# A planned attention and gated feed-forward kernel: load order of the first chunk, engine copies of shifted values, early sink scores, float16 normalisation from PSUM, and a last tile in halves

## The chip, the cores and the metric

The kernel runs on one core of a Trainium2 chip. The metric is the device time of one execution in microseconds (us). A core has TensorE (PE in the profile, its weight loads PEld), VectorE (DVE), ScalarE (ACT), GpSimd (POOL) and SyncE (SP). Each engine works through its own instructions in order; POOL and SP issue the DMAs here.

## The reference, cut to what matters

Causal attention over 4 batches, 8 heads, 768 positions and 64 dimensions. Heads 0, 2 and 6 are full ("retrieval"), the other five see a window of 64 positions and 4 sink positions. Its output is the input of a gated feed-forward block with a gated residual.

```python
scores = q @ k.T / 8
keep   = causal if is_retrieval[h] else causal & ((k_pos < 4) | (q_pos - k_pos < 64))
a = exp(scores where keep) ; a = a / sum(a) ; x = a @ v      # x: 3072 tokens x 512
g = x @ w_gate ; val = x @ w_val                             # 512 -> 1536
out = x + sigmoid(x @ w_res) * ((gelu(g) * val) @ w_out)     # 1536 -> 512
```

## The kernel before, in words

The 3072 tokens are worked in six chunks of four tiles of 128 tokens (CHUNKS). A chunk passes three stages: attention (`attention`, `scores`, `sink_scores`, `weigh`, `to_features`), gate and value with gelu (`gate_value`, 96 matmuls of 512 columns at L939), and output (`output`, 16 residual-gate matmuls at L967 and 48 at L973). The attention of the next chunk is woven into the output stage of the one before.

Nothing of the order on an engine is written by hand. Every step is a Task with an engine (or a choice of two, `flex`), an estimated duration, a priority and its dependencies, and `Graph.schedule` lays all of them out in one simulated run before the program is built; what it lays out is the fixed order of instructions on each engine. An engine that stands before an instruction whose data is late holds up all that is behind it. The planner's estimate of when a DMA lands therefore decides what ends up behind what.

Names that the prediction uses:

- POOL issues the loads (L507), which also change float32 to float16: `qks` holds queries and keys, `va` values (65 columns a head, the last one ones), `wg`, `wv`, `wr`, `wo` the weights. For chunks 0 and 1 queries and keys are transposed by TensorE (L596) and copied to `qkt` (L611); from chunk 2 on SP transposes them by DMA (L634).
- `vs` is `va` shifted by 64 positions, needed for windows that begin in the middle of a tile. Two DMAs on SP make it, one for each half of the partitions (L557).
- `vk` holds the values of the four sink positions. Eight small copies make it for each batch, on DVE or ACT (L547).
- A pair of heads has its scores on PE (L721), exponentials on ACT (L737, into `er` or `es`), masks on DVE (L773). Sink scores (L809) and their exponential `ek` (L816) come once in a chunk.
- `weigh` multiplies by the values: windows (L838), full heads (L848), sinks (L861). Then a reciprocal `rcp` (L887) and the normalisation into the float32 tile `xtok` (L894).
- `to_features` casts `xtok` to float16 `x` (L910), transposes it on PE (L915) and copies it to `xT` (L922), the input of the gate stage. ACT's gelu gives `gact` (L951), DVE's product `hT` (L953).
- In `output`, ACT's tanh gives `srs` (L976), DVE forms `otile` (L978) and adds `xtok` (L981), SP stores (L986).
- Up to 90 idle matmuls on `ident` (L990) fill TensorE's waiting time at the start.

The functions that the change touches:

Of the kernel before, what the change touches and what calls it, by code (L numbers as in the profile page):

```python
# [6 lines left out]
DHEAD = 64  # L7
# [31 lines left out]
VK = ((0, 1), (1, 3), (2, 5), (3, 7), (0, 4), (1, 4), (2, 4), (3, 4))  # L39

class Task:
    __slots__ = ("eng", "dur", "fn", "deps", "order", "prio", "bufs", "fset", "dma",
                 "ndeps", "users", "ready", "end", "done", "pos", "snap", "waits",
                 "signal", "name", "sem", "seq", "grp", "alts", "boost", "mode")

    def __init__(self, eng, dur, fn, deps, prio, bufs=(), fset=None, dma=0.0, order=(), name="", grp=None):
# [15 lines left out]
        self.mode = None  # L62

# [92 lines left out]
class Graph:  # L156
# [23 lines left out]
    def schedule(self):  # L180
# [21 lines left out]
        while left:  # L202
# [3 lines left out]
            for e in ENGS:  # L206
# [74 lines left out]
                for u in t.users:  # L281
# [4 lines left out]
                    u.ready = max(u.ready, (now + dur if t in u.order and t not in u.deps else t.end) + lat)  # L286
# [132 lines left out]
def build_kernel(nc, q, k, v, w_gate, w_val, w_out, w_res, out):  # L419
# [11 lines left out]
    scratch = sb("scratch", [128, 1], FP16)  # L431
    wr = sb("wr", [128, NCB, D_MODEL], FP16)
# [10 lines left out]
    P_x16 = Pool(many("x16", 2, [128, 4, 128], FP16))  # L443
# [9 lines left out]
        "av1": (2, one(0, 1)), "av2": (1, [(0, 1)]),  # L453
        "sc": (2, [(2, 3), (4, 5)]), "scr": (3, one(5, 4, 3, 2)),
        "gv": (4, one(6, 7, 5, 4, 3, 2)), "out": (2, one(6, 7)), "warm": (1, one(7)),
# [21 lines left out]
    def spread(on, prio, dst, src, n, dep):  # L477
        return G.flex({e: (0.3 if e == "dve" else 0.45, lambda e_, e=e: (
            e_.activation(out=dst, in_=src, func=AF.Copy) if e == "act" else e_.tensor_copy(out=dst, in_=src)))
            for e in on}, [dep], prio, name="spread")  # L480

    t_ident = chain(-90, [(128, lambda e: e.memset(ident[:, :], 0.0)),  # L482
                          (128, aff(ident[:, :], ALU.not_equal, 1.0, 0, [[-1, 128]], 1))])

    t_causal = chain(-57, [(128, lambda e: e.memset(m_causal[:, :], 1.0)),
# [11 lines left out]
    t_win = [spread(("dve", "act"), -50, m_win[:, 3:7, :], m_win[:, 1:2, :].to_broadcast([128, 4, 128]), 512, t_win),  # L497
             spread(("dve", "act"), -49, m_win[:, 0, :], m_win[:, 1, :], 128, t_win)]
# [27 lines left out]
    batches = {}  # L526

# [8 lines left out]
    def values(b, a, z, base, each):  # L536
# [5 lines left out]
        if a == 0:  # L542

            def vk(on, sl, j, h):
                def fn(e):
                    o, i_ = at(BB.vk)[32 * j:32 * j + N_SINK, sl, :], at(BB.v)[0:N_SINK, 0, h, :]
                    return e.activation(out=o, in_=i_, func=AF.Copy) if on == "act" else e.tensor_copy(out=o, in_=i_)  # L547
# [17 lines left out]
    def loads_rows(c, si, b, a, z):  # L565
# [11 lines left out]
        for gi, (h0, h1) in enumerate(groups):  # L577
# [6 lines left out]
            if gi == 0:  # L584
                values(b, a, z, base + 2, False)
# [60 lines left out]
    def attention(c, segs, xbuf, xtbuf, xtoks, xttoks):  # L646
        tiles = [(b, i) for (b, a, z) in segs for i in range(a, z)]
        normed, todo = {}, []
# [26 lines left out]
        sinks = sink_scores(c, [t for t in tiles if t[1] > 0], todo[-1].pr)  # L675

        sc = ph(c, "sc")[:-1]
        for t, u in zip(sc[0::2], sc[1::2]) if c else ():
            t.deps += u.deps
            u.order.append(t)  # L680
            for b in u.bufs[:1]:
                t.bufs.append(b)
                b.left += 1
                b.users.append(t)
        for P in todo:
            weigh(P, tiles, sinks, xbuf, xtoks, normed)
            for cb in range(NCB):
                if (2 * cb in normed and 2 * cb + 1 in normed) and cb not in normed.setdefault("cb", []):
                    normed["cb"].append(cb)
                    to_features(c, cb, P.pr, normed, xbuf, xtbuf, xttoks)  # L690

    def scores(P, tiles, banks, g, retr):
# [62 lines left out]
        for xs in ([(0, 1)] if retr[0] == retr[1] else [(0,), (1,)]):  # L755
# [11 lines left out]
            else:  # L767
# [6 lines left out]
                out=split(view()), in0=split(view()), in1=m_, op=ALU.mult))(), txs + mt, pr, bufs=[P.et], name=f"mask{p}")  # L774
# [47 lines left out]
    def weigh(P, tiles, sinks, xbuf, xtoks, normed):  # L822
        n = len(tiles)
        c, pr, heads = P.c, P.pr, P.heads
        av = Buf(P_ps, "av2")
# [27 lines left out]
        def sinkf(x, h):  # L853
            def fn(e):
                r = []
                for lt, (b, i) in enumerate(tiles):
# [3 lines left out]
                    sl = 4 + sinks.four[b, i] if h == 4 else (1, 3, 5, 7).index(h)  # L860
# [5 lines left out]
        if near:  # L866
            deps = []
            for lt, (b, i) in enumerate(tiles):
                deps += [P.ready[x, None, b, i] for x in near] + [batch(b).vtok[i]] + (batch(b).vstok[i] if i else [])
            prev_t = G.add("pe", 0.03 * n * len(near), windows(near, range(n)), deps, pr - 1,  # L870
                           bufs=[P.et, av] + [u for b in both for u in (batch(b).v, batch(b).vs)], name=f"win{P.p}")
# [27 lines left out]
        for h in heads:  # L899
            normed[h] = t2  # L900
# [173 lines left out]
```

## Time and profile before

| what | value |
|---|---|
| median of 3 runs | 290.74 us (290.12 to 291.29) |
| the profiled execution | 290.88 us |
| its span, first to last instruction | 289.1 us |
| PE busy | 271.0 us (94%) |
| ACT, DVE, POOL busy | 144.7, 137.5, 86.3 us |
| mean granted TensorE clock | 0.976 |

The span is cut by the profile's page into 40 slices of 7.2 us; a time "at 85.98" is counted from the span's start. A row of the chain of waits gives a start, a length and what ran or was awaited. A row of the timeline gives start, length, engine, line, operation, tiles, and in brackets how long the engine had stood idle and for whom. A row of the groups gives busy time and the mean duration in ns.

### The profile page before, as it was taken

The numbers are of one execution on the slowest core, as the hardware profiler recorded it, in microseconds if no ns is written. First come the engines' busy times: TensorE is split into PE (matmuls) and PEld (weight loads), VectorE is DVE, ScalarE is ACT, GpSimd is POOL, SyncE is SP. The second block draws the span as 40 slices with busy tenths as digits, with TensorE's granted clock in tenths as the row PEclk, the third lists the DMA queues.
The fourth block names the chain that finished last, engine by engine and source line by source line (L and its number), as shares of the span: only waits on it lengthen the run. The fifth ranks groups of instructions, "written<-read, shape, count | busy, mean of one in ns | idle before, by whom it ended". The sixth has DMA issues, their size and how long they took to land.

```text
span 289.1 us, 5543 instructions
## 1 busy us (share of the span) xinstructions
PE 271.0 (94%) x2334; PEld 136.3 (47%) x2334; DVE 137.5 (48%) x251; ACT 144.7 (50%) x218; POOL 86.3 (30%) x121
## 2 busy tenths in 40 slices
PE   6777999999939999999999999999999999999994
PEld 5544445455413446544445444455444355544441
DVE  2535345367232445763347543457443347643333
ACT  2665436777422477553388433666333667333210
POOL 8999008996390099740000000000000000000000
PEclk9987999999987999999999999999999999999999
DMA  7999999999999999999201100021000011100011
GB/s 84 184 227 207 178 199 212 152 157 132 136 151 231 168 157 128 153 131 201 106 2 40 73 2 0 0 76 39 36 1 2 36 39 39 60 14 2 0 73 73
DMA packets 92489, 28.19 MB, mean 98 GB/s; under 512 B 81200, under 2 KB 88624, under 8 KB 92464
## 3 DMA queue, kind: packets, MB, share of 16 engines
q0 software_dynamic: 70320, 14.69, 61.6%
q1 hardware_dynamic: 22144, 13.15, 22.3%
q8 instruction: 18, 0.29, 0.4%
q14 instruction: 7, 0.06, 0.1%
HBM read 29.36 MB, written 6.29 MB: 123 GB/s over the span
## 4 chain that ended last, share of the span: by engine, by line
PE 85%; DMA 10%; DVE 2%; POOL 2%; issue 1%; ACT 0%; POOLq 0%; DVEq 0%
PE ps L939 41%; PE ps L973 22%; DMA va<-in_v_dram 7%; PE ps L967 7%; PE ps L721 5%; PE ps L848 3%; DMA vs<-va 2%; PE ps L838 2%; PE ps L861 2%; PE ps L915 2%; POOL va L507 1%; PE ps L809 1%; PE ps L596 1%; POOL qks L507 1%; PE ps L990 0%
## 5 line engine op out<-in xcount | busy, mean ns | idle before, releaser
L939 PE MATMUL ps<-xT,wv 128*128 128x512 f16 x288 | 87.7, 387 | 4.6 <-DVE hT L953 4.6
L939 PE MATMUL ps<-xT,wg 128*128 128x512 f16 x288 | 87.7, 387 | 0.6 <-DVE xT L922 0.6
L953 DVE SCALAR_TENSOR_TENSOR hT<-gact,ps 128x512 f16<-128x512 f16 x72 | 49.5, 687 | 75.3 <-ACT gact L951 71.7
L951 ACT ACTIVATE gact<-ps 128x512 f16<-128x512 f32 x72 | 43.0, 597 | 77.6 <-PE ps L939 77.6
L973 PE MATMUL ps<-wo,hT 128*128 128x512 f16 x288 | 70.9, 380 | 0.3 <-ACT srs L976 0.3
L939 PEld LDWEIGHTS ps<-xT,wv 128*128 128x128 f16 x288 | 28.6, 100 | 40.0 <-DVE hT L953 5.4
L939 PEld LDWEIGHTS ps<-xT,wg 128*128 128x128 f16 x288 | 28.4, 100 | 35.1 <-issue 2.2
L737 ACT ACTIVATE er<-ps 128x1024 f16<-128x1024 f32 (+3 forms) x40 | 34.4, 902 | 12.6 <-PE ps L721 12.6
L507 POOL DMA_DIRECT2D qks<-in_k_dram x36 | 28.7, 848 | 34.4 <-DMA qkt<-qks 18.8
L973 PEld LDWEIGHTS ps<-wo,hT 128*128 128x128 f16 x288 | 24.7, 98 | 28.1 <-DVE otile L978 2.0
L507 POOL DMA_DIRECT2D qks<-in_q_dram x36 | 28.9, 852 | 0.3 <-POOL ident L482 0.3
L978 DVE SCALAR_TENSOR_TENSOR otile<-srs,ps 128x512 f32<-128x512 f32 x24 | 16.4, 685 | 20.6 <-PE ps L973 20.5
L967 PE MATMUL ps<-wr,xT 128*128 128x512 f16 x96 | 24.7, 380 | 0.0
L507 POOL DMA_DIRECT2D va<-in_v_dram x24 | 21.3, 912 | 4.4 <-PE ps L861 4.4
L976 ACT ACTIVATE srs<-ps 128x512 f32<-128x512 f32 x24 | 14.3, 596 | 16.6 <-PE ps L967 16.4
L721 PE MATMUL ps<-qkt 64*128 64x64 f16 (+4 forms) x396 | 17.4, 217 | 0.4 <-ACT er L737 0.3
L981 DVE TENSOR_TENSOR otile<-otile,xtok 128x512 f32<-128x512 f32 x24 | 16.5, 688 | 0.6
L894 DVE TENSOR_TENSOR xtok<-ps,rcp 128x512 f32<-128x512 f32 x24 | 16.5, 688 | 0.5
L737 ACT ACTIVATE es<-ps 128x1024 f16<-128x1024 f32 x12 | 12.3, 1022 | 5.7 <-PE ps L721 5.7
L721 PEld LDWEIGHTS ps<-qkt 64*128 64x128 f16 x396 | 10.5, 96 | 8.8 <-issue 4.7
L773 DVE TENSOR_TENSOR es<-es,m_win 128x1024 f16<-128x1024 f16 x12 | 8.1, 679 | 12.8 <-ACT es L737 12.7
L967 PEld LDWEIGHTS ps<-wr,xT 128*128 128x128 f16 x96 | 9.0, 98 | 10.4 <-issue 0.2
(57 smaller groups left out, 191.6 us busy)
## 6 DMA issues: line engine op xcount, KB each, us to landing
out_dram<-otile SPq DMA_DIRECT2D x24, 256.0 KB, 2.0
va<-in_v_dram POOLq DMA_DIRECT2D x24, 128.0 KB, 15.2
qks<-in_k_dram POOLq DMA_DIRECT2D x32, 64.0 KB, 9.2
qks<-in_q_dram POOLq DMA_DIRECT2D x32, 64.0 KB, 9.5
wg<-in_moe_w_gate_dram POOLq DMA_DIRECT2D x3, 512.0 KB, 12.2
wv<-in_moe_w_val_dram POOLq DMA_DIRECT2D x3, 512.0 KB, 13.7
wo<-in_moe_w_out_dram POOLq DMA_DIRECT2D x4, 384.0 KB, 25.2
vs<-va SPq DMA_DIRECT2D x4, 260.0 KB, 6.2
```

The costliest lines, as they stand in the source:

```text
L507: return G.add(eng, issue, lambda e: e.dma_start(out_ap(), in_ap), deps, prio, bufs=bufs, dma=cost, name=name, grp=grp)
L721: return [e.matmul(at(scr)[:, oo:oo + w], lhsT=at(BB.qkt)[half, 1, p, k0:k0 + 128], rhs=at(BB.qkt)[half, 0, p, qq:qq + w], start=True, sto ...
L737: return e.activation(out=o, in_=i_, func=AF.Exp, scale=SM_SCALE)
L894: return e.tensor_tensor(out=o[:, :, :, heads[0] // 4, 64 * (heads[0] % 2):64 * (heads[0] % 2) + 64], in0=avv(0, DHEAD), in1=at(rc)[:, :, ...
L939: return lambda e: [e.matmul(at(dst)[:, :], lhsT=w[:, ci, f * 128:(f + 1) * 128], rhs=at(xtbuf)[:, ci, :], start=(ci == 0), stop=(ci == NC ...
L951: ta = G.add("act", c_act(512), (lambda gb=gb, ga=ga: lambda e: e.activation(out=at(ga)[:, :], in_=at(gb)[:, :], func=AF.Gelu))(), [tg], p ...
L953: th = G.add("dve", c_dve(512), (lambda vb=vb, ga=ga, f=f: lambda e: e.scalar_tensor_tensor(out=at(h)[:, f, :], in0=at(ga)[:, :], scalar=0 ...
L967: e.matmul(at(rb)[:, :], lhsT=at(xtbuf)[:, ci, s], rhs=wr[:, ci, :], start=(ci == 0), stop=(ci == NCB - 1))
L973: e.matmul(at(fb)[:, :], lhsT=at(h)[:, fi, s], rhs=wo[:, fi, :], start=(fi == 0), stop=(fi == NF - 1))
L976: ta = G.add("act", c_act(512), (lambda rb=rb, sr=sr: lambda e: e.activation(out=at(sr)[:, :], in_=at(rb)[:, :], func=AF.Tanh, scale=0.5)) ...
L978: t1 = G.add("dve", c_dve(512), (lambda fb=fb, sr=sr, ot=ot: lambda e: e.scalar_tensor_tensor(out=at(ot)[:, :], in0=at(sr)[:, :], scalar=1 ...
L981: fa = lambda e, ot=ot, lt=lt: e.tensor_tensor(out=at(ot)[:, :], in0=at(ot)[:, :], in1=at(xbuf)[:, lt, :], op=ALU.add)
```

## The change

1. *Load order of chunk 0.* All four loads of queries and keys go out before the four of values; POOL no longer clears `ident` first (DVE does), and makes the mask constants between them. The value loads of chunk 1 go behind `wr` and two parts of `wo`.
2. *Shifted values of chunk 0* are made by two copies on an engine (DVE or ACT by the planner's choice) and not by DMAs.
3. *Sink copies*: four of two heads each take the place of eight. For batch 0 they go to DVE; for later batches the planner reckons with a landing 12 us later than before (`slack`).
4. *Sink scores* get the priority of the second pair of heads, and the scores of the third and fourth pair wait for them in the order.
5. *Normalisation*: for the second pair of each half a float16 tile `x16` is written straight from PSUM (L931 of the changed kernel), and its float32 twin later; the first pair is still cast from `xtok`. Transposes are done for two blocks at a time.
6. *Priorities and order*: masks 90 earlier, pairs weighed one after the other, three PSUM places for chunk 0, the first gate step limited to two PSUM banks, gate steps from the second (chunk 0: third) on ordered behind the transposes.
7. *Idle matmuls*: 70 in place of 90, on a zeroed tile `blank` that DVE sets first.
8. *Last tile* of the last chunk: output matmuls, product, sum and store in two halves of 256 columns.

```diff
-VK = ((0, 1), (1, 3), (2, 5), (3, 7), (0, 4), (1, 4), (2, 4), (3, 4))
+VK = ((1, 4), (3, 4), (4, 5), (4, 7))
...
-                    u.ready = max(u.ready, (now + dur if t in u.order and t not in u.deps else t.end) + lat)
+                    u.ready = max(u.ready, (now + dur if t in u.order and t not in u.deps else t.end) + lat + (u.slack if t.dma else 0.0))
...
+    t_blank = G.add("dve", 0.1, lambda e: e.memset(blank[:, :], 0.0), [], -99, name="blank")
+    t_ident = G.add("dve", 0.1, lambda e: e.memset(ident[:, :], 0.0), [], -98, name="ident")
...
-            BB.vktok = [G.flex({"dve": (0.12, vk("dve", sl, j, h)), "act": (0.25, vk("act", sl, j, h))},
-                               [BB.vtok[0]], base + 1500, bufs=[BB.v, BB.vk], name="vk") for sl, (j, h) in enumerate(VK)]
+            BB.vktok = [G.flex({"dve": (0.3, vk("dve", j, *hs)), "act": (0.35, vk("act", j, *hs))},
+                               [BB.vtok[0]], base + 1500, bufs=[BB.v, BB.vk], name="vk") for j, hs in enumerate(VK)]
+            for t in BB.vktok:
+                t.slack = 12.0 if b else 0.0
+                if b == 0:
+                    t.alts = {"dve": t.alts["dve"]}
...
+        if on_engines:
...
+                ts.append(G.flex({"dve": (c_dve(n_, 3.0, False), vs("dve")), "act": (c_act(n_), vs("act"))},
+                                 [BB.vtok[i - off] for i in range(a_, z)], 130, bufs=[BB.v, BB.vs], name="vs"))
...
-            if gi == 0:
-                values(b, a, z, base + 2, False)
+        values(b, a, z, base + (10 if c == 0 else 5), False, c == 0)
...
-        sinks = sink_scores(c, [t for t in tiles if t[1] > 0], todo[-1].pr)
+        sinks = sink_scores(c, [t for t in tiles if t[1] > 0], 1000 * c + 40 + 5)
...
+        if heads[0] % 2:
+
+            xdeps.append(G.add("dve", c_dve(2 * n * 64), lambda e: e.tensor_tensor(
+                out=at(x16)[:, :, :, half], in0=avv(0, DHEAD), in1=scale(), op=ALU.mult), [t1], pr - 2.5, bufs=[av, rc, x16], name="norm16"))
...
+            last = c == len(CHUNKS) - 1 and lt == 3
+            for w in ((slice(0, 256), slice(256, 512)) if last else (slice(0, 512),)):
...
-    for _ in range(90):
-        G.add("pe", 0.11, lambda e: e.matmul(at(warm)[:, 0:128], lhsT=ident[:, :], rhs=ident[:, :], start=True, stop=True),
-              [t_ident], 1e9, bufs=[warm], name="warm")
+    for _ in range(70):
+        G.add("pe", 0.11, lambda e: e.matmul(at(warm)[:, 0:128], lhsT=blank[:, :], rhs=blank[:, :], start=True, stop=True),
+              [t_blank], 1e9, bufs=[warm], name="warm")
```

Where the instructions stand. POOL at the start of the program, before: the first loads (`qks`, `va`), the unit matrix `ident` and the causal mask.

```order
L482 MEMSET ident 128x128
L507 DMA qks<-in_q_dram 128x4x256
L468 ISA
L468 AFFINE_SELECT ident<-ident 128x128
L507 DMA qks<-in_k_dram 128x4x256
L507 DMA va<-in_v_dram 128x8x64 x4
L485 MEMSET m_causal 128x128
L507 DMA qks<-in_q_dram 128x4x256
L468 AFFINE_SELECT m_causal<-m_causal 128x128
L507 DMA qks<-in_k_dram 128x4x256
```

The same place in the changed kernel, up to the first load of values:

```order
L511 DMA qks<-in_q_dram 128x4x256
L511 DMA qks<-in_k_dram 128x4x256
L471 ISA
L471 AFFINE_SELECT ident<-ident 128x128
L511 DMA qks<-in_q_dram 128x4x256
L511 DMA qks<-in_k_dram 128x4x256
L489 MEMSET m_causal 128x128
L494 MEMSET m_win 128x256
L471 AFFINE_SELECT m_causal<-m_causal 128x128
L471 AFFINE_SELECT m_win<-m_win 128x256
L511 DMA va<-in_v_dram 128x8x64
```

Queries and keys are all out before the first load of values, and four mask steps stand between them; the other three loads of values follow with one mask step between each two.

DVE in chunk 0 before, from the mask of the second pair on:

```order
L773 TENSOR_TENSOR es<-es,m_win 128x1024
L773 TENSOR_TENSOR er<-er,m_win 128x512
L773 TENSOR_TENSOR er<-er,m_causal 128x512
L773 TENSOR_TENSOR es<-es,m_win 128x1024
L887 RECIPROCAL rcp<-ps 128x8
L894 TENSOR_TENSOR xtok<-ps,rcp 128x2x4x64
L910 CAST x<-xtok 128x512
```

The same place in the changed kernel; `vs` are the shifted values, `x<-ps` the new float16 normalisation:

```order
L806 TENSOR_TENSOR es<-es,m_win 128x1024
L921 RECIPROCAL rcp<-ps 128x8
L569 COPY vs<-va 64x1560
L933 TENSOR_TENSOR xtok<-ps,rcp 128x2x4x64
L569 COPY vs<-va 64x1560
L940 CAST x<-xtok 128x8x64
L806 TENSOR_TENSOR er<-er,m_win 128x512
L806 TENSOR_TENSOR er<-er,m_causal 128x512
L921 RECIPROCAL rcp<-ps 128x8
L931 TENSOR_TENSOR x<-ps,rcp 128x8x64
L921 RECIPROCAL rcp<-ps 128x8
L806 TENSOR_TENSOR es<-es,m_win 128x1024
```

DVE now carries both copies into `vs` and the first normalisations between the masks; behind these rows stand a copy into `xT`, two float32 normalisations, a reciprocal, the second float16 normalisation and a copy into `xT`.

DVE in the gate stage of chunk 1, before: `hT` is the product of a gate step, `vk` the sink copy for batch 2, `otile` the next output stage.

```order
L922 COPY xT<-ps 128x512
L953 SCALAR_TENSOR_TENSOR hT<-gact,ps 128x512 x3
L547 COPY vk<-va 4x65 x4
L953 SCALAR_TENSOR_TENSOR hT<-gact,ps 128x512 x9
L978 SCALAR_TENSOR_TENSOR otile<-srs,ps 128x512
```

The same place in the changed kernel:

```order
L1023 TENSOR_TENSOR otile<-otile,xtok 128x512
L987 SCALAR_TENSOR_TENSOR hT<-gact,ps 128x512 x11
L553 COPY vk<-va 4x130 x2
L987 SCALAR_TENSOR_TENSOR hT<-gact,ps 128x512
L806 TENSOR_TENSOR er<-er,m_causal 128x1024
```

The sink copies that stood behind the third gate step stand behind the eleventh of twelve, on DVE and on ACT alike (there behind eleven gelus in place of four).

More of the change, by code (lines that the diff above doesn't have):

```diff
@@ L534, in batch, with values @@
         return batches[b]
[L536 removed]
+    def values(b, a, z, base, each, on_engines=False):
         BB = batch(b)
@@ L684, in attention @@
                 b.users.append(t)
+        last = None
         for P in todo:
[L686 to L690, printed above, removed]
+            if P.heads[0] % 2 == 0:
+                x16 = Buf(P_x16)
+                xdeps = []
+            last, tn = weigh(P, tiles, sinks, xbuf, x16, xtoks, xdeps, last)
+            if P.heads[0] % 2 == 1:
+                for cb in (P.heads[0] // 2, P.heads[1] // 2):
+                    to_features(c, cb, P.pr, x16, xdeps, xtbuf, xttoks)
+                if P is todo[-1]:
+                    tn.order += [t for _, t in xttoks[-2:]]
     def scores(P, tiles, banks, g, retr):
@@ L870, in weigh @@
             prev_t = G.add("pe", 0.03 * n * len(near), windows(near, range(n)), deps, pr - 1,
-                           bufs=[P.et, av] + [u for b in both for u in (batch(b).v, batch(b).vs)], name=f"win{P.p}")
+                           bufs=[P.et, av] + [u for b in both for u in (batch(b).v, batch(b).vs)], order=[last], name=f"win{P.p}")
             prev_t.mode = "col"
@@ L914, in to_features @@
+        return prev_t, t2
+    def to_features(c, cb, pr, x16, xdeps, xtbuf, xttoks):
+        n = 4
         scr = Buf(P_ps, "scr")
         tp = G.add("pe", c_mm(128, n), lambda e: [e.transpose(
-            out=at16(scr)[:, i * 128:(i + 1) * 128], in_=at(x16)[:, i, :], identity=ident[:, :]) for i in range(n)],
-            [tc_, t_ident], pr - 3, bufs=[x16, scr], name="xT")
+            out=at16(scr)[:, i * 128:(i + 1) * 128], in_=at(x16)[:, cb % 2, i, :], identity=ident[:, :]) for i in range(n)],
+            xdeps + [t_ident], pr - 3, bufs=[x16, scr], name="xT")
```

128 lines of the change are left out of this document (75 added, 53 removed).

## The prediction

> **What bounds the kernel now.** I read the page first, then the busy time by stage, then the waits of PE, then the chain at the places where PE stands.
>
> ```profile
> PE 271.0 (94%) x2334; PEld 136.3 (47%) x2334; DVE 137.5 (48%) x251; ACT 144.7 (50%) x218; POOL 86.3 (30%) x121
> ...
> PE 85%; DMA 10%; DVE 2%; POOL 2%; issue 1%; ACT 0%; POOLq 0%; DVEq 0%
> ```
>
> PE is the bound, and DMA holds 10% of the chain. Where, the stages show (columns: stretch, its length, busy time of PE, PEld, DVE, ACT, POOL with instruction counts, granted clock, DMA share, GB/s):
>
> ```profile
> 0.00:26.10 26.10, 17.55 (x319) 13.66 (x320) 11.19 (x25) 15.46 (x24) 25.07 (x42) 0.93 1.25 172
> 26.10:52.00 25.90, 25.34 (x175) 11.94 (x172) 11.55 (x22) 11.47 (x19) 10.27 (x14) 0.94 1.63 195
> 52.00:72.20 20.20, 19.95 (x259) 11.12 (x259) 11.81 (x23) 15.59 (x22) 17.70 (x25) 1.00 1.96 147
> 72.20:100.10 27.90, 23.32 (x99) 9.80 (x96) 8.41 (x15) 8.48 (x17) 10.09 (x14) 0.88 1.78 168
> 100.10:123.70 23.60, 23.60 (x277) 12.59 (x277) 14.52 (x27) 16.58 (x22) 20.73 (x28) 1.00 1.81 147
> 205.50:226.20 20.70, 20.70 (x98) 9.41 (x96) 7.56 (x11) 6.92 (x12) 0.00 (x0) 1.00 0.03 11
> 270.70:289.00 18.30, 14.30 (x64) 5.83 (x62) 6.20 (x9) 2.55 (x5) 0.00 (x0) 1.00 0.15 57
> ```
>
> The first row is the attention of chunk 0, in which PE mostly waits. A gate stage costs 20.70 with 96 matmuls where nothing disturbs it (fifth chunk, sixth row), so 0.216 a matmul; that of chunk 1 (fourth row) costs 27.90 with a clock of 0.88. In the stages of the later chunks PE is busy in all of the time: nothing but fewer or shorter PE instructions helps there. So three places can give: the start, chunk 1's gate stage, and the end.
>
> **Chunk 1's gate stage: the stall and the clock behind it.** The chain there, then PE's timeline:
>
> ```profile
> 69.56 14.76 DMA va<-in_v_dram
> ...
> 85.70 0.23 DVE hT L953
> ```
>
> ```profile
> 80.80 0.59 PE L939 MATMUL ps<-xT,wg 128*128 128x512 f16 x2
> 85.98 1.03 PE L939 MATMUL ps<-xT,wv 128*128 128x512 f16 x2 [4.58 <-DVE hT L953]
> ...
> 90.97 0.60 PE L939 MATMUL ps<-xT,wv 128*128 128x512 f16 x2
> ```
>
> ```profile
> 84.34 1.36 DVE L547 COPY vk<-va 4x65 f16<-4x65 f16 x4 [5.91 <-DMA va<-in_v_dram]
> ```
>
> The values of batch 2 are asked for at 69.56 and land at 84.3. DVE has the sink copies of that batch behind the third gate step and stands 5.91 before them; the products behind them do not come, PSUM stays full, PE stands 4.58. The clock falls: from 85.98 to 90.97 twelve matmuls take 4.99 in place of 12 x 0.216 = 2.59, so 2.40 more. Together 7.0.
>
> The change moves these copies behind the eleventh product. The stage begins at 72.2 and, undisturbed, ends at 100.1 - 7.0 = 93.1; taking off the 3.5 that I give the start (below), at 89.6, and the copies are reached about 1.5 ahead of that, near 88. The values land at about 84 to 86: the stream of loads is a little ahead (two DMAs for `vs` are gone), but two query loads now stand before them. So they are in hand before they are needed, DVE and ACT do not stand, and the clock has no cause to fall. I take the whole **7.0**; with a partial return, 4.
>
> **The start.** The chain there:
>
> ```profile
> 0.80 0.21 POOL ident L482
> ...
> 1.37 0.88 POOL qks L507
> ...
> 5.95 6.67 DMA va<-in_v_dram
> ...
> 12.64 6.35 DMA vs<-va
> ...
> 19.03 0.56 PE ps L838 x16
> ...
> 26.37 3.30 PE ps L939 x8
> 29.67 0.46 PE ps L915 x8
> ...
> 30.15 0.44 DVE xT L922
> ...
> 30.67 0.38 PE ps L939
> ```
>
> Values land at 12.63, the shifted copies at 18.99, and only then does the second pair of heads go on; the gate stage runs in earnest from 30.67. By then 8 of its matmuls are done; the change allows 4 (two PSUM banks), so the point to compare is 30.67 - 4 x 0.216 = 29.8.
>
> Loads now. POOL issues the same eight loads, values last; the rows of the last of them before, of PE's value matmuls on the tile that landed last, and of the load's landing:
>
> ```profile
> 7.97 0.81 POOL L507 DMA_DIRECT2D qks<-in_k_dram  x1
> ...
> 13.11 0.68 PE L848 MATMUL ps<-va,er 128*128 128x65 f16 x17
> ```
>
> ```profile
> DMA to landing us min/median/max: 6.6/6.6/6.6
> ```
>
> The eighth load landed at 7.97 + 6.6 = 14.6. POOL's first load goes out at 0.80 and not at 1.37 (no `ident` to clear), so the last values land near 14.0, 1.4 later than before, and queries and keys ahead of them. DVE decides from there, by these durations (groups: busy time, mean ns, idle before; the third row is the cast alone, min/median/max):
>
> ```profile
> L894 DVE TENSOR_TENSOR xtok<-ps,rcp 128x512 f32<-128x512 f32 x24 | 16.5, 688 | 0.5
> L773 DVE TENSOR_TENSOR es<-es,m_win 128x1024 f16<-128x1024 f16 x12 | 8.1, 679 | 12.8 <-ACT es L737 12.7 <-ACT m_win L479 0.2
> L910 DVE CAST x<-xtok x12: 418/426/820, 23.7 to 248.3; 128x512 f16<-128x512 f32 x12
> L887 DVE RECIPROCAL rcp<-ps 128x8 f32<-128x8 f32 x24 | 4.9, 206 | 12.2 <-PE ps L861 7.0 <-PE ps L848 4.9
> L922 DVE COPY xT<-ps 128x512 f16<-128x512 f16 x14 | 5.9, 419 | 7.6 <-PE ps L915 7.4
> L773 DVE TENSOR_TENSOR er<-er,m_win 128x512 f16<-128x512 f16 x6 | 2.5, 422 | 1.4 <-ACT er L737 1.4
> ```
>
> The copy into `vs` (1560 elements) is not in the trace. At the rate of the mask it takes 1560/1024 x 0.68 = 1.0, at the cast's 1560/512 x 0.43 = 1.3; half the mask's, should a copy, with one operand less, run faster, 0.5; twice the cast's, as its slowest one took (0.82), 2.6. I take 1.0. The float16 normalisation I price as the float32 one, 0.69: same operand from PSUM, same count.
>
> From 14.0: the 17 value matmuls 0.7, then reciprocal 0.21, `vs` 1.0, normalisation 0.69, `vs` 1.0, cast 0.5: 18.1. Two masks 0.84, reciprocal 0.21, float16 normalisation 0.69, reciprocal 0.21, mask 0.68, copy 0.42, two normalisations 1.38, reciprocal 0.21, float16 normalisation 0.69: 5.3, so 23.4; a dozen handovers of 0.04 make 23.9. Transposes to first matmul took 29.67 to 30.67, 1.0: 24.9. The masks of the last pair also wait for exponentials on ACT, so I take 25.4. That is 29.8 - 25.4 = 4.4 earlier.
>
> The clock at this place, in windows of 2 us:
>
> ```profile
> 26.00:28.00 2.00, 2.00 (x11) 0.50 1.23 205
> 28.00:30.00 2.00, 2.00 (x13) 0.64 1.45 193
> ```
>
> Half clock lasted about 2 + 1.4 = 3.4 and ended just before the gate stage ran in earnest, so before, most of it was hidden in a wait. The 70 idle matmuls of the change are all placed in the first quarter of this stage, and nothing fills PE's gaps later: a stretch of 3.4 at half clock costs up to 1.7 if it falls after 25.4. I charge half, 0.9. [...]
>
> The start gives 4.4 - 0.9 = **3.5**; bounds 0.5 (`vs` at 2.6 each, a whole cold stretch) and 6 (`vs` at 0.5, no cold stretch).
>
> [...]
>
> What this pulls forward: the output stage of chunk 0, reached at 52.0 before. It needs `wo`:
>
> ```profile
> 22.57 3.04 POOL L507 DMA_DIRECT2D wo<-in_moe_w_out_dram  x4
> ```
>
> ```profile
> DMA to landing us min/median/max: 23.5/25.2/26.9
> ```
>
> The last part lands at about 24.8 + 26.9 = 51.7. In the change it comes after the same loads, less the two `vs` DMAs and the early start: about 50. It is needed some 3.5 into the stage (four matmuls of L967 and eight of L973 at 0.216, about 0.9 of scores between), so at 52.0 - 3.5 + 3.5 = 52. The cover is 2; were the start to gain over 6, this landing would take the rest. The values of chunk 1, now behind `wr` and half of `wo`, are not wanted until its windows, later in the stage.
>
> **The end.**
>
> ```profile
> 282.29 2.78 PE ps L973 x12
> ...
> 285.19 0.70 DVE otile L978
> ...
> 285.91 0.69 DVE otile L981
> ```
>
> After the last matmul product and sum stand in line, 1.39. In halves only the second half remains: between half of 0.69 and, with the reciprocal's 0.21 for 8 columns as the floor, 0.45 each. At 0.45 it saves 0.5, and a store of half the size 0.1: **0.6** (0.4 to 0.9). PE's columns stay the same.
>
> **What costs nothing.** The sink copies (four took 1.36 above) lie beside PE work. Of each chunk's four casts two become float16 normalisations at 0.69: DVE has 14.5 of 23.6 in its fullest later stage. Sink scores early, mask priorities and the order of pairs shuffle PE rows in stages in which PE never waits; the number of matmuls stays. Were the shuffle to open or close gaps, I allow 1 each way.
>
> **Sum.** 3.5 + 7.0 + 0.6 = 11.1. From the profiled execution, 290.88 (span 289.1 and 1.8 outside it, which stays): **279.8**. The median of the runs, 290.74, is 0.1 from it, within their spread.
>
> **The rivals.**
>
> *The start gains nothing* (0.15). DVE carries two copies and two normalisations that the chain of before did not have in this place, and values land 1.4 later. If `vs` takes 2.6 and a cold stretch follows, 3.5 falls to about 0: 283.3. For: DVE works in order, and its casts do reach 0.82. Against: the 6.35 of the DMA copies is gone in any case. [...]
>
> *The stall comes back smaller* (0.12). The sink copies are only moved, and still wait for the same landing. If the values come 3 after DVE and ACT reach them, about 91, the wait costs 3 and the clock's 2.4 again: 279.8 + 5.4 = 285.2. For: the DMA share of that stage is 1.78, and the landing took 14.76. Against: the copies stand eight products later.
>
> *The start gains more, up to `wo`* (0.08): 6 in place of 3.5: 277.3.
>
> *Slower than before* (0.03). The same sink copies, if the batch-2 values land so late that ACT and DVE both stand ahead of chunk 2's exponentials: each us late is a us lost. From a landing near 97 on (88 + 11.1 - 2.4) the gain is eaten; at 100, 293. The load would have to take twice its 14.76.
>
> That the change does not do what it says I exclude: the order shows the copies, loads and halves where it puts them.
>
> **How the numbers follow.** The forecast has 0.62. The range takes in its bounds (start 0.5 to 6, shuffle 1): 276.5 to 284.5, with all of the first and third rivals and the smaller part of the second. About 0.5% is what a measurement of this kernel can tell from no change, here 1.45. Faster by more: 0.62 + 0.15 + 0.12 + 0.08 = 0.97, less 0.01 for a stall and a lost start together: 0.96. Within: 0.01. Slower: 0.03.
>
> **What would show it.** Right: no wait of PE for `hT` in chunk 1's gate stage and clock 1.00 there; that stage at about 20.9; the long run of gate matmuls starting at 25.4; `vs` copies near 1.0; the last DVE pair at 0.45 each; later stages within 0.5 of before. Wrong: a DVE or ACT wait for `va` late in chunk 1, PE waiting for `wo`, or a later stage with a clock under 1.

## The result: 280.5 us, 10.4 less than before

The changed kernel takes 280.47 us in the median of 4 runs (279.84 to 280.81), beside 290.88 of the kernel before (290.12 to 291.29): a ratio of 0.964, 95% interval 0.962 to 0.967. The profiled execution took 280.51 with a span of 278.8; that of before 290.88 with 289.1. The forecast was 279.8. The sum came out near; its terms did not, and the experiments are about them. Run again later beside the experiments, the changed kernel gave 0.9636 (0.9611 to 0.9660); below I use 0.964 for it, and turn differences of ratios into us with 291.

The page of the changed kernel, busy time and the chain's shares:

```profile
PE 269.9 (97%) x2326; PEld 137.9 (49%) x2326; DVE 142.3 (51%) x256; ACT 138.6 (50%) x203; POOL 86.0 (31%) x120
...
PE 91%; DVE 3%; DMA 2%; POOL 2%; issue 1%; ACT 0%; POOLq 0%
```

DMA has fallen from 10% of the chain to 2%. By stage (columns as in the prediction; these are the start, chunk 0's gate stage, chunk 1's gate stage, the fifth chunk's and the end):

```profile
0.00:26.70 26.70, 21.52 (x312) 16.41 (x312) 14.93 (x35) 14.45 (x20) 25.17 (x41) 0.74 1.27 165
26.70:49.00 22.30, 22.23 (x160) 10.64 (x164) 9.45 (x14) 9.90 (x16) 10.11 (x14) 1.00 1.61 194
...
71.30:91.60 20.30, 20.30 (x101) 9.01 (x100) 9.82 (x17) 7.45 (x15) 9.27 (x12) 1.00 1.69 171
...
197.70:218.40 20.70, 20.70 (x102) 9.28 (x102) 9.46 (x15) 7.35 (x13) 0.00 (x0) 1.00 0.04 13
261.40:278.80 17.40, 14.22 (x77) 7.07 (x74) 6.52 (x11) 2.62 (x5) 0.00 (x0) 0.98 0.16 60
```

Chunk 1's gate stage is 20.30 long with a clock of 1.00, where it had 27.90 with 0.88. But the start shows a clock of 0.74, lower than before's 0.93: TensorE ran at half clock from 11.80 to 25.46.

DVE at the end of chunk 1's gate stage, changed kernel:

```profile
90.15 0.69 DVE L987 SCALAR_TENSOR_TENSOR hT<-gact,ps 128x512 f16<-128x512 f16 x1 [1.04 <-ACT gact L985]
90.85 0.39 DVE L553 COPY vk<-va 4x130 f16<-4x130 f16 x2
91.88 0.69 DVE L987 SCALAR_TENSOR_TENSOR hT<-gact,ps 128x512 f16<-128x512 f16 x1 [0.63 <-ACT gact L985]
```

The sink copies start without any wait: the first values of batch 2, which they read, had landed at 85.25, over 5 us before.

To see where the time went, I take the last gate matmul (the last row of each stage on PE) of chunks 0, 1 and 5. Before:

```profile
51.47 0.59 PE L939 MATMUL ps<-xT,wv 128*128 128x512 f16 x2
...
99.61 0.59 PE L939 MATMUL ps<-xT,wv 128*128 128x512 f16 x2
...
270.07 0.59 PE L939 MATMUL ps<-xT,wv 128*128 128x512 f16 x2
```

Changed (the gate matmul is now L973):

```profile
48.44 0.59 PE L973 MATMUL ps<-xT,wv 128*128 128x512 f16 x2
...
91.05 0.59 PE L973 MATMUL ps<-xT,wv 128*128 128x512 f16 x2
...
260.83 0.59 PE L973 MATMUL ps<-xT,wv 128*128 128x512 f16 x2
```

These rows have a trap. Between two gate stages before, the number of output matmuls was not the same: the planner had let some of them slide past the next gate stage. The groups of PE from 144.1 to 162.1 before, and from 134.3 to 155.3 in the changed kernel, both the attention of the fourth chunk:

```profile
L973 PE MATMUL ps<-wo,hT 128*128 128x512 f16 x36 | 9.1, 380 | 0.0
```

```profile
L1016 PE MATMUL ps<-wo,hT 128*128 128x512 f16 x48 | 12.2, 380 | 0.2
```

That stage seems 3.0 longer after the change (21.0 in place of 18.0), and 2.6 of it are twelve matmuls of 0.216 that had only been put elsewhere. Counted between the gate stages in the same way, 6 of chunk 0's 48 were outstanding at the end of chunk 1's gate stage before (1.3), and none at the end of chunk 5's. So corrected:

| part | before | changed | gain | forecast |
|---|---|---|---|---|
| up to chunk 0's last gate matmul | 51.5 | 48.4 | 3.0 | 3.5 |
| from there to chunk 1's | 48.1 + 1.3 | 42.6 | 6.8 | 7.0 |
| from there to chunk 5's | 170.5 - 1.3 | 169.8 | -0.6 | 0 |
| to the end of the span | 19.0 | 18.0 | 1.1 | 0.6 |

In these two executions every term seems right within half a us or so. The third experiment shows that the first line owes a good part of its 3.0, by two other profiles of the old start 1.6 and 2.6, to the execution of before that was profiled.

### The profile page after: what moved, and what is told of

Same layout as the page of the kernel before. It is cut to its first block, busy times and chain, and to the rows that moved or that the text cites. A ratio compares the mean times of both kernels' runs of the same rounds, so it can differ in the third digit from the quotient of the medians.

```text
span 278.8 us, 5525 instructions
## 1 busy us (share of the span) xinstructions
PE 269.9 (97%) x2326; PEld 137.9 (49%) x2326; DVE 142.3 (51%) x256; ACT 138.6 (50%) x203; POOL 86.0 (31%) x120
## 4 chain that ended last, share of the span: by engine, by line
PE 91%; DVE 3%; DMA 2%; POOL 2%; issue 1%; ACT 0%; POOLq 0%
PE ps L973 45%; PE ps L1016 23%; PE ps L1001 7%; PE ps L754 5%; PE ps L881 3%; PE ps L871 2%; DMA va<-in_v_dram 2%; PE ps L948 2%; PE ps L895 2%; PE ps L621 1%; POOL qks L511 1%; DVE xtok L933 1%; PE ps L842 1%; DVE vs L569 1%; ACT xT L955 0%
## 5 line engine op out<-in xcount | busy, mean ns | idle before, releaser
L973 PE MATMUL ps<-xT,wg 128*128 128x512 f16 x288 | 85.8, 381 | 0.5 <-ACT xT L955 0.5
L973 PE MATMUL ps<-xT,wv 128*128 128x512 f16 x288 | 85.5, 380 | 0.0
L1016 PE MATMUL ps<-wo,hT 128*128 128x512 f16 (+1 forms) x300 | 71.9, 371 | 0.2
L973 PEld LDWEIGHTS ps<-xT,wv 128*128 128x128 f16 x288 | 28.3, 98 | 34.3 <-issue 0.5
L973 PEld LDWEIGHTS ps<-xT,wg 128*128 128x128 f16 x288 | 27.8, 98 | 33.4 <-ACT xT L955 0.8
L1016 PEld LDWEIGHTS ps<-wo,hT 128*128 128x128 f16 x300 | 25.8, 98 | 27.7 <-DVE otile L1020 3.2
L1020 DVE SCALAR_TENSOR_TENSOR otile<-srs,ps 128x512 f32<-128x512 f32 (+1 forms) x25 | 16.6, 662 | 24.6 <-PE ps L1016 24.6
L754 PE MATMUL ps<-qkt 64*128 64x64 f16 (+4 forms) x396 | 18.3, 221 | 0.4 <-ACT ek L849 0.3
L1023 DVE TENSOR_TENSOR otile<-otile,xtok 128x512 f32<-128x512 f32 (+1 forms) x25 | 16.5, 661 | 0.5
L881 PE MATMUL ps<-va,er 128*128 128x65 f16 x252 | 12.1, 199 | 2.2 <-DMA va<-in_v_dram 2.2
L1001 PEld LDWEIGHTS ps<-wr,xT 128*128 128x128 f16 x96 | 8.7, 98 | 10.4 <-ACT gact L985 0.5
## 6 DMA issues: line engine op xcount, KB each, us to landing
wv<-in_moe_w_val_dram POOLq DMA_DIRECT2D x3, 512.0 KB, 12.6
```

What stands on the lines that cost most here:

```text
L754: return [e.matmul(at(scr)[:, oo:oo + w], lhsT=at(BB.qkt)[half, 1, p, k0:k0 + 128], rhs=at(BB.qkt)[half, 0, p, qq:qq + w], start=True, sto ...
L881: return [e.matmul(at(av)[:, o:o + 65], lhsT=at(P.et)[:, P.where[x, kt, b, i]:P.where[x, kt, b, i] + 128], rhs=at(batch(b).v)[:, kt, heads ...
L973: return lambda e: [e.matmul(at(dst)[:, :], lhsT=w[:, ci, f * 128:(f + 1) * 128], rhs=at(xtbuf)[:, ci, :], start=(ci == 0), stop=(ci == NC ...
L1001: e.matmul(at(rb)[:, :], lhsT=at(xtbuf)[:, ci, s], rhs=wr[:, ci, :], start=(ci == 0), stop=(ci == NCB - 1))
L1016: e.matmul(at(fb)[:, w], lhsT=at(h)[:, fi, s], rhs=wo[:, fi, w], start=(fi == 0), stop=(fi == NF - 1))
L1020: t1 = G.add("dve", c_dve(n), (lambda fb=fb, sr=sr, ot=ot, w=w: lambda e: e.scalar_tensor_tensor(out=at(ot)[:, w], in0=at(sr)[:, w], scala ...
```

## The experiments

All ratios are to the kernel before, run beside them on the same chip. "Give or take" stands for the 95% interval. After each edit the planner lays the program out again, so that instructions elsewhere can change their place too.

### The sink copies alone, from both sides

*Late sinks*: before, and only the slack.

```diff
+            for t in BB.vktok: t.slack = 12.0 if b else 0.0      # eight copies, as before
```

> The kernel before with one thing of the change: for later batches the planner reckons the sink copies' data 12 us later (the slack), so that seven of the eight copies for batch 2 stand on DVE behind the tenth product of chunk 1's gate stage and one on ACT behind the tenth gelu. Theory (the stall of 4.6 and the half clock of 2.4 behind it come from the place of these copies alone): no wait of PE for hT in that stage, clock 1.00, the time falls by about 7.0, from 290.7 to about 283.8. Rival (the stage got shorter by the rest of the change, such as the earlier start, the order of the loads or the gate steps held behind the transposes): the wait stays or returns one or two products later, 286 to 290.5.

Measured: 282.6 us, ratio 0.9714 (0.9682 to 0.9746): 8.3 less than before, with an interval of 7.4 to 9.3. PE's instructions and both DMA issuers' stand in the order of before; only DVE and ACT have rows in other places. PE has no wait in the stage; the stretch of 71.30 to 90.95 of this kernel:

```profile
71.30:90.95 19.65, 19.65 (x93) 8.91 (x91) 8.79 (x18) 6.75 (x13) 9.23 (x13) 1.00 1.76 167
```

*Early sinks for batch 2*: the changed kernel, and the slack gone for that batch alone. Two copies change their place on DVE and two on ACT, nothing else.

```diff
-                t.slack = 12.0 if b else 0.0
+                t.slack = 12.0 if b not in (0, 2) else 0.0
```

> The changed kernel with the slack taken away for batch 2 alone; only four copies move on DVE and ACT, from behind the eleventh to behind the fourth product of chunk 1's gate stage. DVE would reach them at about 79, the values land at about 85.3. Theory: DVE and ACT stand some 6, PE some 5 (it can run ahead by two steps), and the clock falls to half for about 2.4 of loss: 280.5 + 7.0 = about 287.5. Rival (the copies' place is not what decides): under 282. Between: a stall of 5 without a fall of the clock gives 285.

Measured: 288.47 us, ratio 0.9910 (0.9877 to 0.9943): 7.8 more than the changed kernel, give or take 1.2. The copies on DVE, then PE, timelines of this kernel:

```profile
87.05 0.74 DVE L553 COPY vk<-va 4x130 f16<-4x130 f16 x2 [8.02 <-DMA va<-in_v_dram]
```

```profile
80.96 0.59 PE L973 MATMUL ps<-xT,wv 128*128 128x512 f16 x2
88.34 1.03 PE L973 MATMUL ps<-xT,wg 128*128 128x512 f16 x2 [6.79 <-ACT gact L985]
89.17 1.06 PE L973 MATMUL ps<-xT,wv 128*128 128x512 f16 x2
```

Stall and half clock are back, PE's wait now with ACT as its name, since two of the copies stand there behind the fourth gelu. Both sides agree: the place of these copies is worth about 8. The stall ends with a landing and not with work. Chunk 0 ended 3.0 earlier here than in before's profile (48.66 and 51.69, the starts of its last gate matmul), but the copies stand one product later, so DVE reached them at 79.0 (78.4 before); the values came at 87.0 (84.3 before), 17.4 after their load was issued in place of 14.8, and PE's wait grew from 4.58 to 6.79. So the size of the stall is that of a landing, which differs from one profile to the next: between the last gate matmuls of chunks 0 and 1 the late sinks save 6.3 against before, and the early sinks cost 9.1 against the changed kernel.

### The last tile in one piece

```diff
-            last = c == len(CHUNKS) - 1 and lt == 3
+            last = False
```

> The changed kernel with the last tile in one piece of 512 columns. Theory (product and sum of half the width save 0.5, the store of half the size 0.3, the rest is PE's order at the end): 1.0 more, about 281.4; the last DVE pair takes 0.69 each. Rival (the tail's 1.1 come from elsewhere, the halves cost PE what they save on DVE): within 0.3 of 280.4.

Measured: 281.56, ratio 0.9701 (0.9681 to 0.9721): 1.8 more, give or take 0.9. The chain's end in the changed kernel, and with the whole tile:

```profile
273.04 2.63 PE ps L1016 x24
...
275.69 0.43 DVE otile L1020
...
276.15 0.42 DVE otile L1023
```

```profile
272.71 2.78 PE ps L1016 x12
...
275.61 0.70 DVE otile L1020
...
276.33 0.69 DVE otile L1023
```

The pair saves 0.54; after it the span goes on for 2.2 with a half store and 2.5 with a whole one; and PE's row is 0.15 shorter for 24 half matmuls than for 12 whole ones. That makes 1.0. Here the profiles are firmer than the ratio: from the start of chunk 5's last gate matmul to the end of the span it is 17.72 to 17.75 in all eleven profiles with halves and 18.83 or 18.84 in the three without, so the end is worth 1.1, near the low end of what the ratio gives.

### How much is the start worth?

*Sinks and halves*: before with the slack and the changed output function, without the change's start, early sinks, normalisation and order.

```diff
+            for t in BB.vktok: t.slack = 12.0 if b else 0.0
-    def output(...):      # as before
+    def output(...):      # as changed
```

> The kernel before with the 12 us of slack for the sink copies and with the changed kernel's output function (last tile in halves), and nothing of the change's start, early sinks, normalisation or order. By the prediction (start 3.5): 3 to 3.5 slower than the changed kernel, about 283.8. By the theory after the runs so far (the profiled execution of before had a start that was 2.6 slower than the same instructions in the run with the late sinks; the start edits together are worth about 1): 281 to 282.

Measured: 282.11 (280.23 to 283.62), ratio 0.9698 (0.9664 to 0.9731): 1.7 slower than the changed kernel, give or take 1.2, and not 3.5. The late sinks (0.9714) beside the whole tile (0.9701), equal at both ends and different in start and order, give 0.4, give or take 1.1. The 3.5 lie outside both intervals.

Why did the profiles show 3.0? In the start, both of these kernels have before's instructions in before's order, on every engine. The first chunk's gate matmuls and the start of the long run in the chain, of the run with late sinks and then of the one with sinks and halves:

```profile
25.25 1.80 PE ps L939 x8
...
28.05 5.12 PE ps L939 x23
```

```profile
24.67 3.35 PE ps L939 x8
...
29.02 7.07 PE ps L939 x32
```

Before it was 26.37 for the eight (3.30 long) and 30.67. So with before's start the long run begins anywhere from 28.05 to 30.67. Two things differ from one execution to the next: the last values landed at 11.32 in the late-sinks run and at 12.63 in before's, and the eight matmuls took 1.80 at full clock and 3.30 where half clock fell on them. The old start has done four gate matmuls more by then, worth 0.9. So against the late-sinks run (28.05 less 0.9) the changed kernel's 26.77 is a gain of 0.4; against the other, 1.4. The changed start is a draw too: the row stands at 26.20 to 26.88 in the four profiles that have it as it is.

### Which part of the start gains, which loses

Four corners: loads of values early (as before) or last, shifted values by DMA or by copies. All else is as in the changed kernel.

```diff
-        values(b, a, z, base + (10 if c == 0 else 5), False, c == 0)
+        values(b, a, z, base + (2 if c == 0 else 5), False)            # old start: early, DMA
+        values(b, a, z, base + (10 if c == 0 else 5), False)           # shift by DMA: last, DMA
+        values(b, a, z, base + (2 if c == 0 else 5), False, c == 0)    # old loads, copies
```

> The changed kernel with the start's loads as before: values behind the first group of queries and keys, shifted values of chunk 0 by two DMAs again. Everything else stays (four sink copies, early sink scores, float16 normalisation, halves). Theory (the start's 3.0 come from the shifted values no longer passing through a DMA of 6.35): about 283.5. Rival A (they come from the float16 normalisation and the new order of masks and pairs): within 1 of 280.5. Rival B (the old load order also delays or advances chunk 1's values and with it its stage): over 285.

> The changed kernel with only the shifted values of chunk 0 made by two DMAs again; the loads keep the new order, values last. Theory: the values land at 15.1, a DMA of about 6.35 makes the shifted ones at about 21.5, where two copies on DVE had them at 19.2; the windows of the second pair start about 2.2 later, some of it beside other work: 281.5 to 283. Rival (the DMA's time lies beside DVE's masks and normalisations, which are freed of two copies): within 0.4 of 280.4.

> The changed kernel with the values of chunk 0 loaded behind the first group of queries and keys again, and the shifted values still copied on DVE: the fourth corner beside the changed kernel (new loads, copies), the old start (old loads, DMA) and the new loads with the DMA. Theory (the late values are what the new load order costs, about 4 of landing; the copies are worth about 2 by themselves): the copies run at about 15.5, the second pair's windows at about 17, the long gate run begins at 24 to 25 and the time is 277.5 to 279, under the old start's 279.0. Rival (DVE, with two copies and the normalisations in line, is the bound wherever the values land): 280 or more.

| ratio (us) | values early | values last |
|---|---|---|
| by DMA | 0.9588, 0.9566 to 0.9610 (279.0) | 0.9715, 0.9689 to 0.9741 (281.8) |
| by copies | 0.9569, 0.9546 to 0.9591 (278.43) | 0.964 (280.5), the changed kernel |

Undoing the load order and the copies together makes the kernel faster, by 1.5, give or take 1.0, where I had expected it 3 slower. The new load order costs 2.0, give or take 1.0, with the copies (0.9569 and 0.9636, measured side by side) and 3.7, give or take 1.0, with the DMA. The copies give 2.2 back, give or take 1.0, where the values come last, and 0.6, give or take 0.9, where they come early: there no gain is shown. The copies with the old loads have the lowest ratio, but these runs can't tell them from the old start. The chain of the changed kernel in the start, then of the copies with the old loads:

```profile
7.09 6.06 DMA va<-in_v_dram
...
15.75 0.90 PE ps L881 x14
...
18.21 1.01 DVE vs L569
...
19.27 0.65 PE ps L871 x16
...
24.41 1.44 PE ps L973 x4
...
26.77 3.41 PE ps L973 x15
```

```profile
3.34 3.48 POOL va L511 x4
...
12.00 0.64 PE ps L881 x17
...
16.11 0.84 DVE vs L569
...
17.00 0.44 PE ps L871 x16
...
22.47 1.86 PE ps L973 x4
...
25.19 4.97 PE ps L973 x23
```

With values last, the first pair's value matmuls (L881) end at 16.7 and DVE does reciprocal, copies and normalisation only then; with values early they end at 12.6, and DVE has the first pair behind it when the copies come at 15.5. The windows (L871) start 2.3 earlier. In this start PE waits 1.4 in all for queries and keys, which the new order brings forward, and not at all for values; in the changed kernel it waits 2.2 for values and 0.3 for queries. With values last and the DMA, the two latencies stand in line (the chain of that run):

```profile
9.16 6.16 DMA va<-in_v_dram
...
15.33 7.18 DMA vs<-va
...
22.55 0.65 PE ps L871 x16
```

This profile, at 283.7, is the slowest of its six runs; the ratio above is of all of them.

### Sink scores and masks

```diff
-        sinks = sink_scores(c, [t for t in tiles if t[1] > 0], 1000 * c + 40 + 5)
+        sinks = sink_scores(c, [t for t in tiles if t[1] > 0], todo[-1].pr)
-        for t in ph(c, "sc")[:-1]: ...                # third and fourth pair wait for the sinks
-                ... txs + mt, pr - 90, ...
+                ... txs + mt, pr, ...
```

On the changed kernel, then on the old loads with copies:

> The changed kernel with the sink scores late again (priority of the last pair, no order between them and the scores of the third and fourth pair) and the masks without their 90. Theory (PE never waits in the later stages, the shuffle is worth nothing there; in chunk 0 up to 0.5 either way): within 0.7 of 280.4. Rival (these two edits carry part of the start's 3.0): 281.5 or more, with the loss ahead of the first long gate run.

> The old load order with the copies on DVE (278.4), with the sink scores late and the masks without their 90 again. If these two edits carry the start's gain by themselves (they cost 2.3 where the values are late): 280.5 to 281. If they matter only where the values land late, since the sink scores then fill PE's wait: within 0.7 of 278.4.

Measured: 282.73, ratio 0.9735 (0.9711 to 0.9759), 2.8 slower than the changed kernel, give or take 1.0, where my theory said within 0.7; and 281.09 (278.01 to 282.02), ratio 0.9632 (0.9596 to 0.9669), 1.8 slower than its own base, give or take 1.2. The edits that I costed at nothing gain more than the whole start does net. The loss is in the start: in the profiles chunk 0's last gate matmul starts at 51.87 in place of 48.66, and at 50.55 in place of 46.91 on the old loads, and from there to chunk 5's last it is 211.9 to 212.6 in all kernels made from the changed one but the early sinks. (Both profiles with the old order are the slowest of their six runs.) Waits of PE up to 33 us, with the old order on the changed kernel:

```profile
PE ps L973 <- DVE rcp L921: 1.0, 1, 1.0
...
PE ps L895 <- ACT ek L849: 0.8, 1, 0.8
```

Neither wait is in the changed kernel: late sink scores make the sink matmuls (L895) wait for their exponential, and on DVE the cast and the second float16 normalisation come behind masks, just ahead of the gate stage. The latter in the changed kernel, then with the old order:

```profile
24.76 0.69 DVE L931 TENSOR_TENSOR x<-ps,rcp 128x512 f16<-128x512 f32 x1
```

```profile
26.20 0.68 DVE L931 TENSOR_TENSOR x<-ps,rcp 128x512 f16<-128x512 f32 x1
```

Half clock may take part: both profiles with the old order have 17.07 of it in one stretch (13.65 and 6.83 in their bases). By four executions it is not all: on the old loads, at a mean clock of 0.981 or 0.982, the old order took 280.3 and 281.0 and its base 278.7 and 279.2. How much would be left without any half clock is open. Which of the two edits carries more was not tried apart.

### Half clock in the start

```diff
-    for _ in range(70):
+    for _ in range(66):
...
+            G.add("pe", 0.4, lambda e: [e.matmul(at(warm)[:, 0:128], ...) for _ in range(40)], [t_blank], 1e9, order=<scores of pair 0>)
```

On the changed kernel; then, with 30 of them, on the old loads with copies:

> The changed kernel with 40 idle matmuls in the 2 us in which PE waits for the first values (from 9.8 to 12.1), in place of 4; nothing else moves. In the changed kernel the clock was at half from 11.80 to 25.46, over all of the start's work behind that wait. Theory (the half clock on this work is what the start still pays): the clock stays at 1.00, the 16 transposes take 0.64 in place of 1.06, and the long gate run begins 1 to 2 earlier than 26.77: about 279.0. Rival A (the start's chain runs through DVE, ACT and the landing of values, PE's half clock is hidden): within 0.3 of 280.4. Rival B (the idle matmuls hold up the value matmuls behind them): over 280.8.

> As the old loads with the copies, and 30 idle matmuls in place of 4 in the wait for the first values. Theory (half clock on the start's work costs 0.5 to 1): 0.5 to 1 under the old loads with the copies, and executions closer together. Rival (PE's half clock lies beside DVE and ACT): within 0.3 of it.

Measured: 279.73, ratio 0.9640 (0.9622 to 0.9658); and 278.30, ratio 0.9572 (0.9549 to 0.9595). Neither differs from its base (0.964 and 0.9569) by what these runs can tell, 0.9. The first theory's 1.4 is excluded by that, the second's 0.5 to 1 not quite. The clock did change. Windows of PE in the changed kernel, and with the 40 idle matmuls:

```profile
14.00:18.00 4.00, 3.82 (x67) 0.50 1.23 201
18.00:22.00 4.00, 3.55 (x63) 0.50 1.24 207
```

```profile
14.00:18.00 4.00, 2.99 (x72) 1.00 1.23 200
18.00:22.00 4.00, 2.95 (x68) 0.81 1.24 206
```

In the first of these windows PE is busy for 3.8 of 4 at half clock, and for 3.0 at full clock with more matmuls: most of what the clock takes comes out of waits. In the profiles chunk 0's last gate matmul starts at 47.82 in place of 48.66; but without the added matmuls it stands anywhere from 48.09 to 48.77 in four profiles, so this row does not settle it either. All four runs lie within 0.52 (279.51 to 280.03), the five runs of the changed kernel beside the other experiments within 1.58. On the old loads the 30 did not keep the clock up: half clock lasted 10.24 in that profile and 6.83 in its base's (mean clocks 0.982 and 0.988).

*The changed kernel again*, the yardstick:

> The changed kernel as it is, on the same chip and beside the same runs of before as the other two. All theories: a ratio of 0.964 to the kernel before; it is the yardstick for the clock's share in the start. [...]

Measured: 280.6 (279.59 to 281.17), 0.9636.

## Why the prediction was right in the sum and wrong in the start

- **Chunk 1's gate stage, 7.0: right in kind, 1 too small.** No wait for `hT` or `va`, clock 1.00, 20.3 long where 20.9 was given. Both one-edit runs say about 8 (8.3 and 7.8), with intervals that reach down to 7.4 and 6.6. The 7.0 were read from one execution, whose values landed 14.8 after their issue; in the early-sinks run they took 17.4.
- **The start, 3.5: wrong.** It is worth 0.4 by one pair of runs and 1.7 by another, give or take 1.1 and 1.2. Three steps failed. First, the point to compare, 29.8, is one draw: the same start put the long run at 28.05 and 29.02 elsewhere, so 27.2 and 28.2 by the same reckoning. Second, the load order: I had the last values land at 14.0 and costed that as 1.4 later than before on a chain that the copies shorten. POOL's first load still went out at 1.33 (0.80 assumed), and more mask steps stand between the loads than the prediction counted; the last load of values went out at 9.16 (7.97 for the eighth load before) and landed at 15.10. The long run began at 26.77 in place of 25.4, and 1.1 of these 1.4 can come from the landing. That was a size. The larger error is that I had asked whether the copies beat the DMA and not whether the values had to come late at all; they had not, and this costs 2.0. Third, "sink scores early, mask priorities" stood under what costs nothing, argued from later stages in which PE never waits. In the start PE does wait, and there these edits gain 1.8 to 2.8. The second and third error, a loss and a gain, nearly cancel, and that they do is luck. In a row, from sinks and halves to the changed kernel: all but loads and copies gains 3.2 (give or take 1.2; 0.9698 to 0.9588), the late loads lose 3.7, the copies give back 2.2. So nearly the forecast of 3.5 comes from edits that had mostly been priced at nothing.
- **The pieces of the start.** The float16 normalisation took 0.69 as priced; what it gains was not tried apart, nor were the remaining priorities and orders of the change. The copies took 0.56 and 1.01, for 1.0 each. `wo`'s last part landed at 50.7 (about 50 said), and PE did not wait for it. The half clock came, but as one stretch of 13.65 ahead of the long run and not behind it. Of the 0.9 charged for it nothing was seen in the times, but they could not have told 0.9 from nothing.
- **The end, 0.6: a little small.** 1.1: the pair as said (0.43 and 0.42), the store 0.3 in place of 0.1, and 0.15 on PE.
- **Later stages within 0.5 of before: only once counted rightly.** Single stages differ by up to 3.0; with the output matmuls put back where they belong, all four later chunks together lose 0.6. That is inside the 1 allowed.
- **The sum.** By the runs 8 + 1.2 + 1.1 = 10.3, taking 1.2 for the start, between its two values, and 9.7 with the 0.6 that the later chunks lose; measured 10.4, forecast 11.1. A start 2 too large, a stall 1 too small and an end 0.5 too small made it near, and that is luck. One figure of the rivals is a slip: by the sums there, a landing at 100 gives 279.8 + 12 + 2.4 = 294 and not 293. The rival "the start gains nothing", 283.3, named the right term; its mechanism (copies of 2.6 and half clock) was not what took the gain.

What stays open: how much the chance of the clock is worth. In the last run of the old order with early loads one execution had a mean clock of 1.00 and took 278.01; the other five had 0.970 to 0.982 and took 280.3 to 282.0. That is more than the idle matmuls gained anywhere. It is one execution, so it shows no cause.

## What to carry to other kernels

A gain read off one profiled execution against another is only as good as the stage's repeatability: run the same instructions again, or a kernel with an edit that leaves the stage alone, before a term is taken from it. In this case the same start ended anywhere within 2.6 us. A load put earlier puts another later; ask of each which of them the chain waits for, and try the corners apart, since a good edit (copies in place of DMAs, early sink scores) can hide the cost of a bad one made with it. Where a scheduler may move work over a stage's border, count the instructions of the stage before comparing its length.

## What the runs showed of the hardware

- The two copies of `vs` are of one shape, 64x1560 from SBUF to SBUF. Over the nine kernels that make them on DVE, eight copies took 0.56 and ten took 0.83 to 1.01 (in the changed kernel the first 0.56, the second 1.01; with the old loads 0.56 and 0.83; with the 40 idle matmuls 0.98 and 1.01). In the changed kernel and with the old loads POOL was issuing loads beside them all the time; in the changed kernel:

```profile
16.92 1.91 POOL L511 DMA_DIRECT2D qks<-in_k_dram  x2
```

In both, the long copy began while a load was being issued and ended 0.37 to 0.39 behind the end of that issue: here from 18.21 to 19.22, with the issue's end at 18.83; with the old loads to 16.95, with the end at 16.58. The short copy of the changed kernel began at 16.91, within 0.03 of an issue's end (16.94). What makes a copy long is not shown: no run here has the copies without loads in the program.
- Up to the last us of the span, half clock came in stretches of 3.41 and its multiples: in the profile of before 3.41 twice and 6.83, in the changed kernel's 13.65, with the 30 idle matmuls on the old loads 10.24 in all (mean clock 0.982), with the old order 17.07 (mean clock 0.970 in both profiles). Over starts of the same instructions they came at other moments: before from 19.18 to 22.59 and from 26.01 to 29.42, with the late sinks about 3.4 in all between 20 and 26 (clock 0.73 in 20 to 24, 0.68 in 24 to 26). What starts and ends a stretch is not shown, and PE's busy time alone (by records whose ends are modelled) does not tell: cut at steps of 3.41, the four windows of 11.80 to 25.46 in the changed kernel hold 2.80, 3.13, 3.06 and 3.07 of PE's work, and only behind the last did the full clock come back. With the 40 idle matmuls the work of 14 to 18 began at full clock and kept it (clock 1.00 in 10 to 14 and in 14 to 18).
